# Key tiles in two halves of 64 rows in a fused sparse attention and long convolution

## The chip, the cores and the metric

The kernel runs on one core of a Trainium2 chip. The metric is the device time of one execution in microseconds (us), as the median of several. TensorE (PE) multiplies matrices, VectorE (DVE) and ScalarE (ACT) work element by element, GpSimd (POOL) and SyncE (SP) here mostly issue transfers. A matmul on TensorE has a stationary operand, loaded ahead as weights, and a moving one that streams through; its result goes to PSUM, which the program uses as eight banks of 512 32-bit columns.

## What is computed

An attention with 8 global keys and a local window of 96, and then a gated long convolution. Sizes: B = 4 batches, H = 8 heads, S = 768 positions, D = 64.

```python
scores = (q @ k.T) / sqrt(D)
rel = pos[:, None] - pos[None, :]
is_global = pos[None, :] < 8
is_local = (rel >= 0) & (rel < 96)
dist = where(is_global & ~is_local, 96, abs(rel))
a = softmax(where(is_global | is_local, scores - slope[h] * dist, -1e9))
x = heads_side_by_side(a @ v)                      # (4, 768, 512)
x1, x2, x3 = split(x @ w_proj)
conv = irfft(rfft(x2, axis=1) * rfft(filter_fft, axis=0), axis=1)
out = (x1 * conv * x3) @ w_out
```

So a query needs at most 96 local keys and 8 global ones.

## The kernel before

**Attention.** Keys are cut into seven tiles of 112 rows. Each tile stands in 128 partitions: the 8 global rows first (8 more rows are zero), then 112 keys of its own. A key can be seen by queries up to 95 positions after it, so a tile of 112 keys meets 112+96 = 208 query columns (the last tile 96). For each head pair `scores` (L681) multiplies the transposed keys `KT` (64 rows of one head, 128 columns) with 208 columns of the transposed queries `QT`: L711. The two heads of a pair stand in rows 0 to 63 and 64 to 127. ScalarE takes the exponential into `E` (L739), VectorE multiplies by a mask of decay and window (L751). In batch 0, where the masks come late, the distances are instead added on TensorE before the scores, as products with a diagonal matrix of slopes (`biases`, L686 to L699).

`values` (L754) then works on query tiles that begin at the same places as the key tiles, 112 apart and 128 wide: seven tiles, each with one product with its own key tile (L769) and one with the tile before (L774), 128 rows and 65 columns (64 of v and a column of ones for the sum). VectorE takes the reciprocal (L799) and scales into `xn` (L793); `transpose_x` (L804) turns it on TensorE (L815) or the transfer engines turn it (`crossed_x`, L822), into `xT`. The queries and keys are transposed on TensorE too: in 16 bits by `turned` (L661, L668), the first tiles of batch 0 in 32 bits by `turned32` (L629, L635), some in batch 3 by transfers (`crossed`, L651).

**Loads.** GpSimd's queue loads q, k and v tiles with a change of type (`load_rows`, `load_run`, `load_q`); the first q and k tiles come in 32 bits on SyncE's and ScalarE's queues (`first_tiles`). The global rows of v are copied to all tiles on SyncE's queue (`load_global`), in batch 0 by VectorE or ScalarE from rows that were loaded apart (`first_rows`, L1148).

**Convolution.** Gates (L860), projections (L934), a forward transform (L622), products with the filter's spectrum, an inverse transform (L959, L962), and the output projection (L986), all with weight tiles of 128 x 128.

**Order.** The methods record operations with the tiles that they read and write. `Plan.schedule` (L152) places them in the order that the string `ORDER` (L40) writes out by hand or by a planner: number of the operation, engine, PSUM banks. Each engine works strictly through its own part of that list. A word such as `i17b0` is 17 matmuls on an idle tile (`busy`, L300), at the start.

Of the kernel before, what the change touches and what calls it, by code (L numbers as in the profile page):

```python
# [16 lines left out]
P = 128  # L17
NG = 8
KL = 112
LO = P - KL  # L20
HUGE = 1.0e5
# [19 lines left out]
4V 0S 1A 2S 3A 30V 9G 32A 31A 14V 13V 11V 10A 33V 22G 34V 23V 60A 62A 12V 27V 5V 65A 36G 39G 19S 35A 15V 25V 24G 63A  # L41
16V 40G 18V 42G 41G 59A 45G 28V 8V 26V 46G 48G 29A 47G i17b0 74P0 75V 61A 70P1 72P2 71V 68P3 69V 84P45 64A 106P0 76P1
37G 58A 92P67 73A 79A 78A 93P 88P23 77V 94P 85P 38G 108P1 89P 49G 86P 107A 66V 90P 95A 44G 43G 109V 112P0 113V 87A
110P1 111V 80P67 81P 82P 20V 91A 51G 67V 120P01 83A 114P45 121A 152P2 153V 50G 154P3 155V 118P67 158P0 115A 159V 119A
156P2 157V 17V 116P45 21V 117A 160P67 161A 162P23 163A 96P45 97V 98V 101P01 166P67 167A 164P45 122P23 52G 102V 103V
123V 127P01 104P6 124V 128V 53G 129V 7G 217P7 165A 105A 99P4 168P23 125P6 130P5 258G 100V 218A 126A 212P4 131A 173P01
137P5 132P6 169V 170V 171P2 213A 219V 220V 221A 174V 175V 176P7 138P3 259G 172A 357P0 214V 215V 133P2 134A 267G 266G
216A 224P6 177V 199V 198V 206V 139V 385P7 184P4 358A 55G 135V 255G 189P5 140A 141V 386V 179P7 225A 257G 355P3 256G
264G 226A 183P0 265G 359A 6A 353P1 191A 201V 143P5 227V 181A 136V 194P7 56G 57G 185A 200V 202V 356V 383P0 228V 229A
205V 260G 186A 354V 208V 230A 223V 361P23 145A 203V 196A 367P45 362A 364P67 384V 178P1 207V 148P0 365A 295P2 204V 360V  # L50
368A 180V 396P45 150A 296A 397A 390P67 209V 210V 211V 187V 363V 370P01 371A 391A 293P3 294A 270G 369V 291P2 280P0 366V
387P67 222V 292A 398V 388A 231V 232V 233V 234V 393P45 299P3 300A 394A 54G 281A 282P2 283A 429P1 273G 306P3 307A 278P6
279A 147P7 149A 286P2 372V 261S 235V 236V 272G 287A 389V 142P3 433P6 434A 271G 431P7 144A 263G 430A 485G 237V 373P45
262S 151V 268G 297P2 298A 240P6 484G 241A 182V 193P3 195A 374V 432V 238P2 239A 392V 243P6 244A 269G 375V 395V 378P01
486G 379V 380V 435P45 436A 487G 197V 438P23 439A 404P67 405V 146V 376P0 496G 406V 245P1 246A 377V 437V 581P4 284P5
285A 444P23 445A 441P67 442A 407P1 188P0 488G 582V 399P45 381P2 408A 440V 585P3 274G 190V 400V 401V 446V 583P0 382A
586V 252P67 254A 253A 275G 276G 495G 584V 402P1 403A 447P45 489G 490S 443V 613P7 614A 248P23 448V 494G 587A 249A 304P6
305A 452P01 410P7 250A 412A 500G 247V 712G 449V 450P2 453V 454V 425P6 451A 251V 501G 455P3 659P7 456V 502G 427A 493G
302V 660A 595P01 589P45 498G 478V 590A 596A 592P23 593A 588A 414P6 458P7 499G 727G 468P4 416A 301V 661P5 308V 711G
460A 303V 242V 729G 594V 409P0 657P1 658V 611P2 309V 288V 612A 289V 424P6 426A 428V 477V 479V 290V 411A 470A 662A  # L60
473P1 475A 420P7 422A 415P6 413V 312P4 480V 313A 320P5 725G 417A 324P1 472P0 321V 474A 669P23 325A 598P67 599A 523P4
481V 714G 510P1 670A 316P5 314P0 192V 511A 600V 672P23 621P67 317V 524A 715G 482V 812P1 315A 591V 673A 322P4 323A 622A
310P0 311A 813V 730G 814A 418V 419P5 318P1 319A 597V 506P4 507A 421V 491S 463P5 465A 624P67 618P01 619A 666P23 457P4
667A 519P5 674V 625A 483V 508P0 663P23 881S 615P67 713G 326V 327V 328V 329V 623V 330V 520A 664A 462P1 423V 509A 620V
720G 728G 497G 616A 521P5 492G 606P23 505G 333V 334V 464A 467P0 469A 522A 607V 601P67 466V 277G 602V 608V 459A 626V
350P1 810P5 514P0 665V 351A 716G 347P4 603A 503G 835S 671V 525P1 526A 348A 476V 344P2 717S 722G 811V 837S 504G 527P5
345A 515A 528A 617V 668V 632P67 331V 604P4 605A 678P23 532P0 633V 634V 533A 679V 512P5 513A 680V 332V 808P1 627P67
628V 882S 534P0 675P45 676V 609P2 809A 629V 535A 610A 635P1 335P3 677V 630P2 631V 529V 636A 721G 836S 471V 336A 724G
530V 883S 821P01 822A 818P67 819A 820V 815P45 816A 726G 880S 723G 838S 516V 338P3 839V 652P2 654A 681S 339A 642P6 644A
817V 648P7 531V 846P45 517V 682S 840P23 683S 650A 847A 518V 823V 824P01 825A 826V 647P6 841A 643P7 645A 638P4 640A  # L70
719G 827P01 828V 884V 341P5 829V 342A 649A 646V 653P7 849P01 850A 536V 732G 537V 461V 651V 705V 891P45 343S 892A
888P23 704V 851V 637P6 544P0 689P1 707V 639A 655A 545A 548P4 731G 691A 549A 550P6 542P5 893V 842V 540P7 543A 706V 352S
538P0 539A 552P1 553A 695P4 551A 641V 700P0 541A 702A 708V 697A 690P1 830P67 546P0 692A 848V 685P4 684P1 831V 832V
889A 687A 843P23 693V 890V 709V 885P67 340S 547A 844A 894P45 733P0 895A 886A 554V 710V 896V 718S 750P2 855P45 856V
# [1174 lines left out]
```

## Time and profile before

| | |
|---|---|
| median of 3 runs | 168.94 us (168.76 to 168.98) |
| profiled execution | 168.69 us, its span 166.8 us |
| TensorE busy in the span | 160.3 us, 1,621 matmuls |
| VectorE busy | 152.9 us, 336 instructions |
| ScalarE busy | 144.9 us, 302 instructions |
| GpSimd busy | 73.6 us, 99 instructions |
| granted TensorE clock | 1.000 |

The span goes from the first to the last instruction on the core; the rest of the execution's time lies around it. "Busy" of TensorE includes the overlap of matmuls that follow each other, so a full row there is not yet an engine at its peak. The groups that belong to attention on TensorE, with mean length of one:

```profile
L711 PE MATMUL bank<-QT,KT 64*128 64x208 f16 x192 | 13.6, 251 | 0.9 <-DVE KT L306 0.7 <-DVE xT L306 0.2
...
L668 PE MATMUL bank<-ident,kn 128*128 128x128 f16 x88 | 6.9, 219 | 0.0
...
L815 PE MATMUL bank<-ident,xn 128*128 128x128 f16 x72 | 6.3, 219 | 0.0
```

### The profile page before, as it was taken

How to read it: one execution, taken by the hardware profiler on the slowest of the kernel's cores; microseconds unless marked ns; L12 is line 12 of the kernel's file. 1: busy time of each engine (PE TensorE's matmuls, PEld its weight loads, DVE VectorE, ACT ScalarE, POOL GpSimd, SP SyncE). 2: the span in 40 equal slices, each digit the busy share in tenths (PEclk: the TensorE clock that was granted, in tenths of full speed). 3: DMA queues.
4: the chain of work that ended last, by engine and by line, in shares of the span. 5: the costliest groups of instructions: out<-in, count | busy, mean ns of one | idle time of the engine just before them, and what ended most of it. 6: DMA issues, size and time to landing. Idle time of an engine off the chain costs nothing.

```text
span 166.8 us, 4251 instructions
## 1 busy us (share of the span) xinstructions
PE 160.3 (96%) x1621; PEld 99.8 (60%) x1621; DVE 152.9 (92%) x336; ACT 144.9 (87%) x302; POOL 73.6 (44%) x99
## 2 busy tenths in 40 slices
PE   7999999999999999999999989999999999999990
PEld 2566787664567876666457746765744844575430
DVE  5898979999999999999999979999999999999950
ACT  4589979999999998999999998999896788696731
POOL 7999999973889934999570000000000000000000
PEclk9999999999999999999999999999999999999999
DMA  5999999999999999999999990804052104300685
GB/s 121 193 141 127 130 171 166 169 208 181 169 164 154 155 150 63 92 140 149 158 157 130 125 130 19 265 5 118 17 132 51 63 4 181 137 0 0 246 317 194
DMA packets 92916, 22.06 MB, mean 132 GB/s; under 512 B 85760, under 2 KB 89824, under 8 KB 92896
## 3 DMA queue, kind: packets, MB, share of 16 engines
q0 software_dynamic: 75952, 11.95, 100.9%
q1 hardware_dynamic: 14864, 9.33, 23.9%
q10 hardware_dynamic: 2080, 0.52, 1.7%
q8 instruction: 12, 0.20, 0.5%
q14 instruction: 8, 0.07, 0.1%
HBM read 24.94 MB, written 6.29 MB: 187 GB/s over the span
## 4 chain that ended last, share of the span: by engine, by line
PE 58%; DVE 33%; issue 4%; DMA 3%; ACT 0%; DVEq 0%; SPq 0%
PE bank L860 15%; PE bank L986 9%; DVE E L751 8%; PE bank L934 6%; PE bank L959 4%; PE bank L302 4%; DVE xn L793 4%; PE bank L698 3%; DMA KT<-kn 3%; PE bank L711 3%; PE bank L668 3%; PE bank L622 3%; PE bank L769 2%; DVE g L871 2%; PE bank L774 2%
## 5 line engine op out<-in xcount | busy, mean ns | idle before, releaser
L860 PE MATMUL bank<-xT,w 128*128 128x384 f16 x256 | 47.9, 326 | 0.0
L739 ACT ACTIVATE E<-bank 128x832 f16<-128x832 f32 (+2 forms) x64 | 42.8, 759 | 1.1 <-PE bank L711 1.0
L860 PEld LDWEIGHTS <-w 128*128 128x128 f16 x256 | 23.6, 98 | 15.4 <-issue 0.7
L322 POOL DMA_DIRECT2D kn<-in_k_dram x27 | 22.5, 848 | 6.7 <-PE bank L668 4.8
L322 POOL DMA_DIRECT2D vn<-in_v_dram x28 | 24.0, 865 | 2.2 <-DMA w<-in_moe_w_proj_dram 0.9
L986 PE MATMUL bank<-wo,y 128*128 128x512 f16 x96 | 22.9, 379 | 0.1
L751 DVE TENSOR_TENSOR E<-E,mask 128x832 f16<-128x832 f16 (+1 forms) x36 | 21.7, 622 | 0.0
L322 POOL DMA_DIRECT2D qn<-in_q_dram x21 | 18.8, 904 | 3.5 <-PE bank L934 3.2
L310 ACT ACTIVATE ot<-bank 128x512 f32<-128x512 f32 x22 | 12.8, 615 | 5.9 <-PE bank L986 3.8
L793 DVE TENSOR_TENSOR xn<-bank,rc 128x512 f16<-128x512 f32 (+1 forms) x22 | 16.8, 766 | 0.6 <-DVE rc L799 0.2
L310 ACT ACTIVATE ab<-bank 128x512 f16<-128x512 f32 x24 | 14.6, 655 | 1.2 <-PE bank L934 1.2
L869 ACT CAST g<-bank 128x384 f16<-128x384 f32 x30 | 14.5, 523 | 1.2 <-PE bank L860 1.2
L769 PEld LDWEIGHTS <-E 128*128 128x128 f16 x224 | 14.0, 97 | 2.3 <-issue 0.4
L769 PE MATMUL bank<-vn,E 128*128 128x65 f16 x224 | 15.3, 193 | 0.0
L310 ACT ACTIVATE x<-bank 128x384 f16<-128x384 f32 x26 | 13.5, 528 | 2.0 <-PE bank L860 1.3
L986 PEld LDWEIGHTS <-y 128*128 128x128 f16 x96 | 9.1, 98 | 10.1 <-DVE y L1066 0.2
L774 PE MATMUL bank<-vn,E 128*128 128x65 f16 x192 | 15.1, 193 | 0.0
L711 PE MATMUL bank<-QT,KT 64*128 64x208 f16 (+1 forms) x224 | 14.0, 244 | 0.9 <-DVE KT L306 0.7
L306 ACT CAST X<-bank 128x512 f16<-128x512 f32 x24 | 14.2, 643 | 0.3 <-PE bank L622 0.2
L306 ACT CAST eo<-bank 128x384 f16<-128x384 f32 x29 | 13.4, 542 | 0.3 <-PE bank L962 0.3
L774 PEld LDWEIGHTS <-E 128*128 128x128 f16 x192 | 13.2, 97 | 0.5
L711 PEld LDWEIGHTS <-KT 64*128 64x128 f16 x224 | 8.7, 94 | 6.4 <-issue 2.5
(148 smaller groups left out, 337.4 us busy)
## 6 DMA issues: line engine op xcount, KB each, us to landing
out_dram<-ot SPq DMA_DIRECT2D x24, 256.0 KB, 2.4
vn<-in_v_dram POOLq DMA_DIRECT2D x28, 112.0 KB, 5.4
kn<-in_k_dram POOLq DMA_DIRECT2D x27, 112.0 KB, 5.2
qn<-in_q_dram POOLq DMA_DIRECT2D x21, 128.0 KB, 5.6
w<-in_moe_w_proj_dram POOLq DMA_DIRECT2D x4, 256.0 KB, 5.7
g<-in_moe_filter_fft_dram POOLq DMA_DIRECT2D x1, 768.0 KB, 10.2
ot<-in_q_dram ACTq DMA_DIRECT2D x2, 256.0 KB, 6.6
w<-in_moe_w_proj_dram POOLq DMA_DIRECT2D x1, 512.0 KB, 7.2
```

Source lines behind the costliest of these rows:

```text
L306: {"A": nc.scalar.copy, "V": nc.vector.tensor_copy, "G": nc.gpsimd.tensor_copy}[e](out, in_)
L310: self.nc.scalar.mul(out, in_, c)
L322: return self.g.op(eng, 0.57 + 0.00035 * nbytes[0] if eng == "G" else 0.5, lambda _: e.dma_start(dst, src), w=w, r=r, nbytes=nbytes, name= ...
L711: nc.tensor.matmul(bs[hh].f32()[:, off:off + w], self.KT[hs, hp, P * m:P * m + P], self.QT[hs, hp, KL * m:KL * m + w], start=(off == 0 and ...
L739: nc.scalar.activation(dst, src(), Act.Exp, scale=self.scale)
L751: g.op("V", dve(w, 2), lambda _: nc.vector.tensor_mul(eo, eo, mk), r=[("mask", 2 * hp), ("mask", 2 * hp + 1)], w=[("E", hp, gi)], name="ma ...
L769: nc.tensor.matmul(o[:, n, hh], ef[:, at:at + P], vt[:, t, 2 * hp + hh, 0:D + 1], start=first, stop=(t == 0), skip_group_check=True)
L774: nc.tensor.matmul(o[:, n, hh], ef[:, at:at + P], vt[:, t - 1, 2 * hp + hh, 0:D + 1], start=False, stop=True, skip_group_check=True)
L793: nc.vector.tensor_mul(to, o[:, :, :, 0:D].rearrange("p i (t h) d -> p i t h d", h=2), rc.rearrange("p i (t h) o -> p i t h o", h=2).to_br ...
L860: nc.tensor.matmul(bk.f32()[:, 0:h], self.w[:, c, o + P * j:o + P * j + P], self.xT[:, c, h * s:h * s + h], start=(c == 0), stop=(c == 3))
L869: first = g.op("AV", {"A": act(h), "V": 0.0005}, lambda e: nc.scalar.copy(x3, pts[1].f32()[:, 0:h]) if e == "A" else None, use=[pts[1]], w ...
L986: nc.tensor.matmul(bk.f32(), y[:, c, P * t:P * t + P], self.wo[:, c, :], start=(c == 0), stop=(c == 3))
```

## The change

Each tile of 112 keys is now held as two halves of 64 rows: 8 global rows and 56 keys of its own, the second half with its keys first and the global rows last. A half meets 56+96 = 152 query columns, which begin where its own keys begin. In tiles 1 and 4 (`SWAP`) the halves are stored in the other order. Scores become four products of 64 x 64 weights, two heads by two halves, into four quarters of two banks; the values become products of 64 rows, one head pair on the upper half and another on the lower, alternating, in two passes (`values` and `values2`). Query tiles for the values are now six, 128 apart. All transposes of q, k and x of 16 bits are two products of 64 rows instead of one of 128. The groups of key tiles are (0,1,2), (3,4), (5,6). The masks, distances and zeroed gaps follow the new layout; v tiles 1 and 4 are loaded in two transfers; the global rows of v are copied on SyncE's queue in every batch. `ORDER` is a new list, which begins the attention of batch 0 with q tile 3 and k tile 2, and uses 12 idle matmuls at the start and two later.

```diff
-    N, LAST, STEP = 208, 96, 224
-    GRP = [(0, 1), (2, 3), (4, 5, 6)]
+    N, LAST, STEP, GAP, LEAD = 152, 96, 272, 120, 56
+    GRP = [(0, 1, 2), (3, 4), (5, 6)]
+    QG = [(0, 1), (2, 3), (4, 5)]
+    SWAP = (1, 4)
...
+        self.at = [[KL * t + HL * (1 - y if t in self.SWAP else y) for y in range(2)] for t in range(7)]
...
     def load_rows(self, what, dst, src, b, t):
+        parts = [(NG, lo, n)] if what[0] == "kn" or t not in self.SWAP else [(NG, lo + HL, HL), (64, lo, HL)]
...
+    def load_global(self, vt, s):
+        for y in range(2):
+            lo = (P - NG) * y
+            self.load("S", vt[lo:lo + NG], vt[NG:2 * NG, 0:1].to_broadcast(
+                [NG, 7, self.H, self.VD]), [("vng", s, y)], (NG * 7, 16 * self.VD), "vglobal",
                 r=[("vn", s, 0), ("vn1", s)])
...
     def turned(self, what, ts, buf):
             for x, t in enumerate(ts):
                 for i in range(4):
-                    nc.tensor.transpose(b.f16()[:, 512 * x + P * i:512 * x + P * i + P],
-                                        buf[:, t, 2 * i:2 * i + 2, :], self.ident)
+                    for y, b in enumerate(bs):
+                        ps, o = slice(64 * y, 64 * y + ks[y]), 256 * x + 64 * i
+                        nc.tensor.transpose(b.f16()[:, o:o + ks[y]], buf[ps, t, 2 * i:2 * i + 2, :], self.ident[ps, ps])
...
     def scores(self, hp, gi, near=False):
                 for hh in range(2):
                     hs = slice(64 * hh, 64 * hh + 64)
-                    nc.tensor.matmul(bs[hh].f32()[:, off:off + w],
-                                     self.KT[hs, hp, P * m:P * m + P],
-                                     self.QT[hs, hp, KL * m:KL * m + w],
+                    for y in range(2):
+                        ks, q0 = P * m + 64 * y, self.at[m][y]
+                        nc.tensor.matmul(bs[hh].f32()[64 * y:64 * y + 64, off:off + w],
+                                         self.KT[hs, hp, ks:ks + 64], self.QT[hs, hp, q0:q0 + w],
...
     def values(self, j, c, slot):
+        def run(_, x):
+            todo = [[(hh, n, t) for hh in range(2) for n, t in z] for z in parts]
+            for k in range(max(map(len, todo))):
+                for i, y in ((0, x), (1, 1 - x)):
+                    (hh, n, t), hp, ps = todo[y][k], 2 * j + i, slice(64 * y, 64 * y + 64)
+                    at = self.STEP * t + self.LEAD + P * ts[n] - self.at[t][y]
+                    nc.tensor.matmul(
+                        o[i][:, n, hh], self.E[hp][ps, hh, at:at + P], vt[ps, t, 2 * hp + hh, 0:D + 1],
...
+        g.op("P", cost, lambda _: run(_, 0), acq=bs, r=es + vs, w=[val], name="values")
+        g.op("P", cost, lambda _: run(_, 1), use=bs, r=es + vs, w=[val], name="values2")
...
     def transpose_x(self, j, c):
                 for n, t in enumerate(ts):
-                    o = step * i + KL * n
-                    nc.tensor.transpose(tx[:, o:o + P], self.xn[:, t, 2 * j + i], self.ident)
+                    for y, b in enumerate(bs):
+                        ps, o = slice(64 * y, 64 * y + 64), 128 * i + 64 * n
+                        nc.tensor.transpose(b.f16()[:, o:o + 64], self.xn[ps, t, 2 * j + i], self.ident[ps, ps])
```

Counted in the built programs, TensorE's matmuls go from 1,621 to 2,582; those of the convolution are the same.

## The prediction, made before the result was known

> **What bounds the kernel now.** I read the page first, then the waits of TensorE, then stretches of time, then the order in time at the places that the change touches.
>
> ```profile
> span 166.8 us, 4251 instructions
> ...
> PE 160.3 (96%) x1621; PEld 99.8 (60%) x1621; DVE 152.9 (92%) x336; ACT 144.9 (87%) x302; POOL 73.6 (44%) x99
> ```
>
> Three engines are nearly full, so the page alone doesn't say which one sets the pace. The list of what TensorE waited for does, with the stretches (columns: stretch, length, busy time of each engine, clock, DMA):
>
> ```profile
> PE bank L302 <- DVE idle L372: 1.2, 1, 1.2
> PE bank L711 <- DVE KT L306: 0.7, 1, 0.7
> PE bank L711 <- DVE xT L306: 0.2, 1, 0.2
> ```
>
> ```profile
> 30.00:60.00 30.00, 30.00 (x349) 19.54 (x348) 29.49 (x70) 29.73 (x60) 23.86 (x29) 1.00 2.09 171
> 60.00:90.00 30.00, 29.75 (x297) 18.61 (x296) 29.57 (x60) 29.25 (x65) 20.85 (x25) 1.00 1.90 128
> 90.00:120.00 30.00, 29.31 (x367) 19.72 (x363) 28.80 (x61) 28.51 (x61) 0.00 (x0) 1.00 0.76 101
> 120.00:160.00 40.00, 40.00 (x242) 22.08 (x241) 38.48 (x76) 32.03 (x74) 0.00 (x0) 1.00 0.30 100
> ```
>
> From 30 to 160 us TensorE is busy 129.06 of 130 us. Matmuls overlap, so busy could still hide slack; their pitch (from start to start) tells. These lines are in order of time (start, length, engine, line, weight tile as rows*columns, count):
>
> ```profile
> 29.32 0.50 PE L455 MATMUL bank<-ident,fwd 128*128 128x128 f16 x6
> ...
> 29.75 0.30 PE L458 MATMUL bank<-ident,fwd 128*64 128x128 f16 x4
> ```
>
> ```profile
> 61.29 0.61 PE L668 MATMUL bank<-ident,kn 128*128 128x128 f16 x8
> ...
> 61.83 0.53 PE L711 MATMUL bank<-QT,KT 64*128 64x208 f16 x8
> ...
> 62.53 0.35 PE L711 MATMUL bank<-QT,KT 64*128 64x208 f16 x4 [0.17 <-DVE xT L306]
> ...
> 62.82 2.12 PE L860 MATMUL bank<-xT,w 128*128 128x384 f16 x12
> ```
>
> Eight L668 in 0.61 us, the last one 0.219: a pitch of 0.39/7 = 56 ns at 128 columns. Twelve L860: (2.12-0.326)/11 = 163 ns at 384. So a matmul costs 0.417 ns a column and 2.5 ns: 29.6 ns at 65 columns, 89 at 208, 176 at 416. L711's two heads stand in rows 0-63 and 64-127 and run together: a pair takes 89 ns, not twice that. Summed by this law over the instruction order, all matmuls after the warm-up (L302) stream 146.7 us; the first starts at 7.5 and the last at 162.1 us.
>
> **A cost that no group shows.** The L668 group ends its pitch at 61.29+8x0.056 = 61.74, but L711 starts at 61.83; L711's last pair is through at 62.53+2x0.089 = 62.71, L860 starts at 62.82. About 0.1 us is lost where the shape of the weight tile changes, 64*128 against 128*128, both ways. By the trace's nanoseconds it is 92 to 97 in 40 of the 42 such places (the other two waited for something too). From 128*128 to 128*64 (L455 to L458) it is 93, and back 99. Before has 48 such places in its instruction order: 4.6 us. So of the 154.6 us from the first to the last matmul, 146.7 are stream, 4.6 changes of shape, and only 3.3 waiting: TensorE's own stream is the bound.
>
> **The change part by part**, as TensorE's time.
>
> *Removed.* Scores L711: 96 pairs of 208 columns at 89.2 ns and 16 of 96 at 42.5: 9.24 us. Bias L698: 8 pairs of 208, 20 of 416, 8 of 96: 4.57. Values L769 and L774: 416 x 29.6 = 12.31. Transposes of q and k, L668: 160 x 55.8 = 8.93; of x, L815: 72 x 55.8 = 4.02; in 32 bits, L635: 16 at (1.91-0.273)/15 = 109 ns, 1.75. Sum 40.82.
>
> *Added*, by counts in the new instruction order. Scores are fours of 64*64 tiles: 96 of 152 columns and 16 of 96. No row shows four together. Low bound: they stream as one, 65.8 ns. High: L458's first pair, whose matmul lasted 243 ns and not 219, so 24 ns of a 64-column weight load were exposed, each time: 90 ns, +2.7 us in all. L458 had just come through a change of shape, and its second pair lasts 219 again; so I take 65.8, and 24 ns at each of the 35 entries into that shape: 7.00+0.84. Bias: fours, 8 of 304 columns, 8 of 152, 4 of 96: 1.73. Values: 896 matmuls of 64 rows, 448 pairs. Low bound 29.6 ns a pair, high 59 (one after the other); L698's pairs of 96 columns, the nearest row, start 42 ns apart, which is their streaming, so I take 29.6: 13.26. Transposes: 172 pairs of 64 columns at 29.2, 5.02; of x, 64 pairs, 1.87; in 32 bits, 12 pairs at 56 and four at 96 ns, 1.05. Sum 30.77. So the streams save 10.05 us.
>
> *Changes of shape.* Scores are 64*64 now, values and transposes 64*128, everything of the convolution 128*128, and the new order weaves them closely (a run of four L960 between two runs of twelve scores, for example). The new order has 163 such places, 115 more: 118 between 128 rows and 64, 39 between the two shapes of 64 rows, and the few of L447 to L466. 115 x 0.096 = +11.04. Those 39 are the weak point: bounds 0 and 3.7 us; I take the full price, as L455 to L458 also kept its rows and changed its columns alone.
>
> The Trainium skill bears on this: "TensorEngine Tiling (Array Packing)", section Key Properties, says that changing the tiling mode, not merely the tile, drains the engine, and lists 64x64 and 64x128 as two modes. By it the 39 places cost the full 3.7 us, by the most hopeful reading of the rows nothing; the trace agrees with the rule wherever it shows a change, at 92 to 99 ns.
>
> *Filler.* Two of the warm-up matmuls now stand in mid-run: 2 x 0.216 = +0.43. Twelve and not seventeen at the start fill a wait and count nothing.
>
> *Start.*
>
> ```profile
> 7.52 1.91 PE L635 MATMUL bank<-p,ot 128*128 128x128 f32 x16
> ```
>
> ```profile
> L322 POOL DMA_DIRECT2D qn<-in_q_dram x3: 888/893/895, 4.3 to 8.4; - x3
> ...
> DMA to landing us min/median/max: 4.0/4.4/4.7
> ```
>
> Now the first work is L635 on tiles that SyncE and ScalarE asked for. In the new order it is the transposes of q tile 3, GpSimd's second load, then k tile 2; L635's successors are queued behind. GpSimd's preparation before its loads is about as long, so the load goes out at 4.3 and lands at 8.7: 1.2 us later. The new first v tile then has to cross a second DMA (its eight global rows copied to all tiles on SyncE's queue, in place of L1148's copies), and all values wait for that. Bounds 0 (the stage waits for copies anyway) to 1.5; I take +0.9. VectorE's new zeroing of E (four copies of 1,440 elements) hides in that wait.
>
> *Relief elsewhere.* ScalarE's exponentials shrink from 2,688 to 2,016 elements a head pair: by L739's rows (0.815 ns an element, 209 ns each) 48.6 us to 39.8. L751's masks: 22.4 to 18.7. xn (L793): seven tiles a batch to six, -2.2. On engines that TensorE doesn't wait for this is worth at most the 0.94 us not busy between 30 and 160; I take -0.3. GpSimd gets eight more loads (two half tiles of v a batch), 8 x 0.865 = 6.9 us; it ends near 83 us and had 8 us of waiting for buffers that TensorE still held, which hides them.
>
> *Sum:* -10.05+11.04+0.43+0.9-0.3 = +2.0 us. The profiled execution took 168.69 (span 166.8 and 1.9 around it): 170.7. The median shown is 0.25 above it, 168.94: 171.0.
>
> **Rivals.**
>
> *A change between the two 64-row shapes is free, since the split of the rows stays.* Then 39 x 0.096 = 3.7 us fall away: 167.3, faster. It decides from about 21 of the 39 free. For it: before shows no such place. Against: L455 to L458 also kept its rows, and paid.
>
> *Small matmuls don't pair.* 65-column pairs need four instructions, two weight loads and two matmuls, in 29.6 ns. Before never asks for that for long: its values use two, its 96-column pairs four in 42. If 21 ns a matmul is a floor, 448 pairs lose 12.4 ns, 236 lose 12.8, and 96 fours 18: 5.6+3.0+1.7 = +10.3, 181.3; each nanosecond a pair is 0.68 us. For it: L442 and L444, of one column each, start 25 and 28 ns before their successors. Against: the members of a pair start as near as 4 ns.
>
> The Trainium skill, "TensorE: Matmul & The Clock Gate", section "Wait — 56ns, not 53.3ns?", gives a floor of about 25 ns from start to start however small the matmul; taken for each member of a pair that would be an estimate of 50 ns a pair, and some 14 us more. The pairs of 96 columns, 42 ns for two, already go under it, so it gets no more weight than the row gave.
>
> *TensorE only looks like the bound, VectorE's 92% paces it.* Its work falls by 3.7+2.2 us and the end with it: 163. Against: the three waits above, 2.1 us in all.
>
> *The four score tiles don't run at once*, so the change doesn't do what it says: at worst two by two, 96 x 66+16 x 42 = +7.0, 178.
>
> **How the numbers follow.** Forecast 0.55, own range 169.2 (no late start, 0.9 relief) to 173.7 (score weight loads exposed). Free changes between 64-row shapes 0.17; VectorE 0.05. Pairs with a floor 0.13, fours that don't run at once 0.04, and a start that stalls longer 0.06 (173 to 175). What 0.2% tells from no change is 0.34 us. Faster: 0.17+0.05+0.02 of the forecast's edge = 0.24; same 0.05; slower 0.71. The range reaches down to free changes, 167.0, and up to 8 ns lost a pair, 176.5.
>
> **What would show it.** TensorE still above 95% busy; 96 ns at changes of shape, and as much between scores and values; L798's pairs 30 ns apart, L742's fours 66; the first transposes near 8.7 us; ScalarE and VectorE less busy with no gain from it. I am wrong if the scores-to-values places lose nothing, if pairs take 40 ns, or if the end moves with VectorE's work.

## The result, and the profile after

The changed kernel takes 186.32 us (median of 4 runs, 184.79 to 186.80) against 168.85 us before (168.48 to 168.98): a ratio of 1.102, 95% interval 1.096 to 1.109. It is slower, as forecast, but by 17.5 us and not by 2, and lies outside the range (167.0 to 176.5). The profiled execution took 186.80 us, span 185.0; before it was 168.69. (Ratios in this document leave out executions that took over 1.5% more than the fastest of the same kernel; medians, ranges and the profiled execution of early_q_whole don't, so the two can differ by a per cent.)

The page of the changed kernel (whole span; then busy tenths and granted clock in 40 slices of 4.6 us):

```profile
span 185.0 us, 6176 instructions
PE 169.3 (91%) x2582; PEld 96.1 (52%) x2582; DVE 152.1 (82%) x344; ACT 135.5 (73%) x289; POOL 78.1 (42%) x106
PE   7499965899998999999999799999999999999990
PEclk9965599799999999999999999999999999999999
```

TensorE is at 91%, not above 95%. ScalarE is 9.4 us less busy than before and VectorE 0.8 us, without any gain. And the clock row has something that the kernel before has nowhere after its first microseconds: slices of 5 and 6. The stretches say more (columns as in the prediction: stretch, length, busy time of PE, PEld, DVE, ACT, POOL, clock, DMA):

```profile
10.00:24.00 14.00, 13.29 (x254) 8.49 (x258) 7.99 (x24) 9.08 (x19) 13.85 (x19) 0.51 1.75 137
24.00:34.00 10.00, 5.86 (x254) 4.53 (x247) 3.78 (x10) 5.34 (x11) 9.61 (x13) 1.00 2.21 162
34.00:38.00 4.00, 4.00 (x71) 2.41 (x64) 2.53 (x7) 2.71 (x5) 3.12 (x5) 0.57 1.72 185
60.00:100.00 40.00, 39.47 (x713) 22.13 (x712) 37.49 (x83) 35.57 (x75) 27.48 (x34) 1.00 1.52 106
110.00:140.00 30.00, 29.87 (x473) 17.59 (x472) 28.74 (x60) 21.52 (x53) 0.00 (x0) 1.00 0.26 65
140.00:180.00 40.00, 39.99 (x242) 21.97 (x241) 36.57 (x73) 29.83 (x64) 0.00 (x0) 1.00 0.32 114
```

The same columns of the kernel before, in its first stage:

```profile
10.00:20.00 10.00, 10.00 (x168) 6.96 (x166) 8.79 (x25) 9.50 (x16) 10.00 (x13) 1.00 2.04 131
20.00:30.00 10.00, 9.96 (x169) 7.46 (x164) 8.82 (x21) 8.83 (x17) 10.00 (x14) 1.00 1.93 164
```

From 60 us on TensorE is as full as before, but for one wait of 1.2 us at 105 us. More than half of the loss sits ahead of 40 us: 14 us in which it looks busy at half clock, then 10 us in which it works only 5.86. What it waited for (total, times, longest):

```profile
PE bank L798 <- issue: 4.5, 3, 2.4
PE bank L691 <- DMA qn<-in_q_dram: 2.9, 2, 2.5
```

"issue" is a wait that no semaphore explains. Two of its three places, in order of time:

```profile
26.86 0.37 PE L798 MATMUL bank<-vn,E 64*128 64x65 f16 x13 [1.17 <-issue]
27.16 0.30 PE L727 MATMUL bank<-eo 64*64 64x152 bf16 x8
...
29.71 0.69 PE L798 MATMUL bank<-vn,E 64*128 64x65 f16 x33
32.78 0.28 PE L798 MATMUL bank<-vn,E 64*128 64x65 f16 x7 [2.38 <-issue]
```

Both stand in the middle of one values operation, between two matmuls on tiles that were there. In the same lines the change of shape can be read: the last of the thirteen L798 starts at 26.86+0.37-0.19 = 27.04 and has 0.03 us to stream, L727 starts at 27.16, 0.09 later.

Summed over all matmuls of the two profiled executions, from the first real matmul to the last: streaming 146.44 us before, 138.33 after (-8.1); changes of shape, at up to 96 ns, 4.51 and 15.29 (+10.8); the rest, waits and the surplus at half clock, 3.66 and 17.55 (+13.9). The first real matmul starts at 9.04 and not 7.52 (+1.5). Together +18.1, the whole difference. The first gate matmul (L860, now L882), which closes the first stage, comes at 35.99 us and not 25.39: 10.6 of the 18.1 us are lost by then. By the same sums, the stage between these two matmuls streams 12.3 us and not 15.3, has 3.7 us of changes of shape and not 1.7, and 11.0 us of the rest and not 0.9. Behind it the streams save 5.0 us (131.2 to 126.2), but the changes of shape cost 8.7 more (2.8 to 11.5) and the rest 3.8 more: there the change loses without any help from the clock.

### The profile page after: what moved, and what is told of

It is laid out like the page before. It is cut to its first block, busy times and chain, and to the rows that moved or that the text cites. A ratio compares the mean times of both kernels' runs of the same rounds, so it can differ in the third digit from the quotient of the medians.

```text
span 185.0 us, 6176 instructions
## 1 busy us (share of the span) xinstructions
PE 169.3 (91%) x2582; PEld 96.1 (52%) x2582; DVE 152.1 (82%) x344; ACT 135.5 (73%) x289; POOL 78.1 (42%) x106
## 4 chain that ended last, share of the span: by engine, by line
PE 70%; DVE 11%; POOL 5%; issue 4%; ACT 4%; DMA 4%; POOLq 0%; DVEq 0%
PE bank L882 21%; PE bank L1012 12%; PE bank L960 8%; PE bank L798 7%; PE bank L629 6%; PE bank L985 5%; DMA qn<-in_q_dram 4%; PE bank L742 3%; PE bank L691 3%; POOL kn L329 2%; PE bank L838 2%; DVE E L778 2%; PE bank L727 1%; POOL qn L329 1%; DVE pp L565 1%
## 5 line engine op out<-in xcount | busy, mean ns | idle before, releaser
L882 PE MATMUL bank<-xT,w 128*128 128x384 f16 x256 | 49.7, 330 | 0.0
L772 ACT ACTIVATE E<-bank 128x304 f16<-128x304 f32 (+3 forms) x64 | 34.4, 610 | 6.8 <-PE bank L742 6.7
L329 POOL DMA_DIRECT2D vn<-in_v_dram x36 | 28.2, 796 | 9.0 <-DMA g<-in_moe_filter_fft_dram 2.9
L882 PEld LDWEIGHTS <-w 128*128 128x128 f16 x256 | 22.7, 98 | 15.5 <-issue 0.5
L329 POOL DMA_DIRECT2D kn<-in_k_dram x27 | 22.6, 844 | 10.3 <-PE bank L691 9.7
L798 PE MATMUL bank<-vn,E 64*128 64x65 f16 x896 | 21.0, 193 | 4.8 <-issue 4.5
L798 PEld LDWEIGHTS <-E 64*128 64x128 f16 x896 | 16.6, 95 | 13.0 <-issue 11.3
L778 DVE TENSOR_TENSOR E<-E,mask 128x608 f16<-128x608 f16 (+1 forms) x36 | 18.0, 517 | 0.0
L742 PE MATMUL bank<-QT,KT 64*64 64x152 f16 x448 | 16.3, 246 | 0.9 <-ACT E L772 0.6
L818 DVE TENSOR_TENSOR xn<-bank,rc 128x512 f16<-128x512 f32 x23 | 15.7, 688 | 0.5
L317 ACT ACTIVATE ot<-bank 128x512 f32<-128x512 f32 x21 | 12.4, 614 | 4.7 <-PE bank L1012 4.3
L313 ACT CAST eo<-bank 128x384 f16<-128x384 f32 x29 | 12.8, 509 | 2.2 <-PE bank L988 1.5
L742 PEld LDWEIGHTS <-KT 64*64 64x64 f16 x448 | 10.0, 114 | 8.4 <-issue 6.3
L1012 PEld LDWEIGHTS <-y 128*128 128x128 f16 x96 | 8.8, 98 | 10.3 <-DVE y L1092 0.5
L313 ACT CAST X<-bank 128x512 f16<-128x512 f32 x23 | 13.0, 595 | 1.0 <-PE bank L629 1.0
L629 PE MATMUL bank<-ab,fwd 128*128 128x512 f16 x40 | 11.5, 382 | 0.0
L985 PE MATMUL bank<-inv,X 128*128 128x256 f16 x64 | 11.3, 273 | 0.1
## 6 DMA issues: line engine op xcount, KB each, us to landing
g<-in_moe_filter_fft_dram POOLq DMA_DIRECT2D x1, 768.0 KB, 10.1
```

The costliest lines, as they stand in the source:

```text
L313: {"A": nc.scalar.copy, "V": nc.vector.tensor_copy, "G": nc.gpsimd.tensor_copy}[e](out, in_)
L317: self.nc.scalar.mul(out, in_, c)
L329: return self.g.op(eng, 0.57 + 0.00035 * nbytes[0] if eng == "G" else 0.5, lambda _: e.dma_start(dst, src), w=w, r=r, nbytes=nbytes, name= ...
L629: self.nc.tensor.matmul(b.f32(), self.fwd[:, f], src(i, t), start=(n == 0), stop=(n == len(terms) - 1))
L742: nc.tensor.matmul(bs[hh].f32()[64 * y:64 * y + 64, off:off + w], self.KT[hs, hp, ks:ks + 64], self.QT[hs, hp, q0:q0 + w], start=(off == 0 ...
L772: nc.scalar.activation(dst, src(), Act.Exp, scale=self.scale)
```

## The experiments

The first theory was: TensorE waits 2.5 us for q after only twelve warm-up matmuls, this lowers its clock, and the half clock costs up to 8.5 us. The second: the waits called "issue" are for instructions. Each set of runs shared runs of the kernel before on its own chip; their medians are 169.71, 170.00, 169.49 and 169.55 us, so ratios compare best. "Late" sums the waits that no semaphore explains at every 256th of TensorE's instructions, weight loads and matmuls counted: 192, 448, 704 and so on (the ones above 0.5 us). after_again is the changed kernel a second time: its trace differs by 1.7 us in the first gate matmul and by 2.8 us in the late instructions, so smaller differences between single traces show nothing by themselves.

| run | us, median (range) | ratio, 95% interval | first gate, us | half clock after the first rise, us | late, us |
|---|---|---|---|---|---|
| changed kernel | 186.32 (184.79-186.80) | 1.102, 1.096-1.109 | 36.0 | 17.1 | 5.0 |
| long_warmup | 183.98 (180.66-185.94) | 1.071, 1.060-1.082 | 33.2 | 10.2 | 1.9 |
| short_start | 184.21 (183.50-186.13) | 1.087, 1.079-1.095 | 35.0 | 13.7 | 2.7 |
| before_short_warmup | 169.84 (168.79-172.69) | 0.999, 0.996-1.003 | 26.0 | 0 | 0 |
| whole_transposes | 183.31 (183.20-184.34) | 1.082, 1.075-1.089 | 34.5 | 6.8 | 1.4 |
| filler_in_slow_window | 185.41 (185.10-185.93) | 1.090, 1.085-1.096 | 35.1 | 13.7 | 3.3 |
| filled_wait | 187.82 (185.87-190.92) | 1.096, 1.089-1.103 | 34.8 | 3.4 | 3.4 |
| fewer_changes | 192.73 (192.16-194.06) | 1.135, 1.129-1.141 | 33.6 | 20.5 | 6.9 |
| before_reordered | 181.71 (181.25-185.03) | 1.068, 1.063-1.074 | 30.3 | 3.4 | 0 |
| after_again | 186.44 (184.04-188.53) | 1.088, 1.080-1.097 | 34.3 | 20.5 | 2.2 |
| early_q | 182.56 (180.97-185.20) | 1.074, 1.066-1.082 | 32.3 | 10.2 | 1.1 |
| early_q_whole | 184.90 (182.59-185.82) | 1.087, 1.077-1.096 | 35.8 | 13.7 | 2.4 |
| dense_pairs | 200.37 (200.00-200.75) | 1.183, 1.174-1.192 | 25.4 | 13.7 | 12.1 |
| held_clock | 188.46 (187.47-191.37) | 1.108, 1.098-1.118 | 36.7 | 10.2 | 6.0 |
| alternating | 190.80 (190.14-191.14) | 1.126, 1.119-1.133 | 25.4 | 0 | 0 |
| grouped | 182.80 (181.95-183.54) | 1.079, 1.072-1.086 | 25.5 | 0 | 0 |

**Is it the wait at the start?** Three runs of the first set vary what stands at the start.

```diff
-30G 31A 29V i12b0 81P01 8V 27A 87P23 50G
+30G 31A 29V i24b0 81P01 8V 27A 87P23 50G
```

> The changed kernel with 24 warm-up matmuls instead of twelve, nothing else: twelve more at 0.216 us fill the 2.53 us that TensorE waits for q at 6.5 to 9.0 us. Theory clock (that wait is what brings the half clock granted at 10.38 to 24.03 and at 34.27 to 37.68 us): the granted clock stays at 1.00 from about 7 us to the end, and a good part of 17.1/2 = 8.5 us comes back, 186.3 to 178-182. Rival load-bound start (in the first 25 us TensorE waits for copies anyway, and the clock costs little): the clock may stay full, but the time stays within 1.5 us of 186.3. Rival activity (the clock falls because the matmuls of the first 25 us are small and spaced, not because of the wait): half clock stays at about 10.4 us and the time stays. On the stalls that no semaphore explains (1.34 us at 26.85, 2.55 at 32.77, 1.16 at 105.41; before TensorE's instructions 704, 960 and 3520, counting weight loads and matmuls): theory instruction supply says that they stand again before instructions 704 and 960, which are now 24 instructions earlier in the program, and not at 3520 unless small matmuls run up to it; rival data says that they stand at the same values operations as now.

Of the wait 1.2 us are left, the clock is up from 4.2 us, and it falls all the same, from 17.9 to 28.1 us (page, clock row):

```profile
PEclk9999558999999999999999999999999999999999
```

The ratio falls from 1.088-1.102 to 1.071. The two executions that it rests on took 180.66 and 182.81 us, about the upper end of the theory's 178 to 182, but not for its reason, since the clock did not stay up. On the instructions the theory of supply was right in kind: the unexplained waits now stand before instructions 960 and 1,216, the latter in the middle of gate work (L882, 1.33 us at 36.0 us), so at steps of 256 in the count and at other operations. The one before 704 did not come again.

```diff
-i12b0 81P01 8V 27A 87P23
+i16b0 77P67 83P4 75P01 8V 27A 84A 76A 87P23 81P01
```

> The changed kernel with the order of its start put back nearer to that of the kernel before: sixteen warm-up matmuls, then the 32-bit transposes of q1, k0 and q0, whose loads land first, and only then k tile 2 and q tile 3. Theory clock: TensorE's first real matmul starts near 7.5 us and not 9.0, no wait above 1 us before it, the granted clock stays at 1.00, and the time falls like that of the long warm-up or up to 1.5 us more: 177 to 182. Rival load-bound start: the first matmul is earlier but the first gate matmul (35.99 us in the changed kernel) stays within 1 us, and the time within 1.5 us of 186.3.

The first real matmul comes at 7.04 us. Then TensorE waits 1.8 us ahead of the transposes of q tile 3, by the trace for ScalarE's copy of earlier queries out of a bank (L313). The clock falls at 12.7 us, and the first gate matmul comes at 35.0 us, between the two traces of the changed kernel (36.0 and 34.3). No gain from the earlier start is shown.

```diff
-48G 29A 47G i17b0 74P0
+48G 29A 47G i8b0 74P0
```

> The kernel before with eight warm-up matmuls instead of seventeen, nothing else, so that TensorE has nothing to do for some 2.5 us before its first real matmul at 7.5 us. Theory clock: the same half clock shows in this kernel, in stretches of 3.4 us from about 10 us on, and it becomes 3 to 9 us slower, 172 to 178. Rival activity (only the small matmuls of the changed kernel lower the clock): the clock is back at 1.00 by about 10 us and the time stays within 1 us of 168.9.

In the kernel before, a wait of 2.1 us at this place costs nothing (page):

```profile
span 167.6 us, 4233 instructions
PEclk9999999999999999999999999999999999999999
```

Its clock rises at 9.7 us and stays. The first theory falls: the clock falls with most of the wait filled (long_warmup), and with a wait left open it stays up once it has risen (here).

**Is it what TensorE does?** Four matmuls of 512 columns go into the slow stretch at two places:

```diff
-91P67 102P 129P01 14V
+91P67 102P i4b0 129P01 14V
-94P 127P01 104P
+94P i4b0 127P01 104P
```

> The changed kernel (twelve warm-up matmuls) with four matmuls of 512 columns on whole 128x128 tiles put ahead of the transposes of two k tiles, at about 12 and 13 us, inside the stretch of half clock (10.38 to 24.03 us). Theory activity (the clock follows how much of a 3.4 us window the array is streaming: the windows after which it fell held 0.41 to 1.34 us of streaming at full clock, those after which it stayed 1.20 or more, and at half clock it came back after windows of 2.33 us or more and stayed down at 1.20 to 2.41): eight matmuls lift the windows from 10.4 us on, the clock comes back near 14 us and not at 24, and the time falls by 1 to 5 us although 1.7 to 3.4 us of matmuls are added. Rival gap (only a wait of TensorE above about 1 us lowers the clock, for a fixed stretch): half clock stays until about 24 us, and the time grows by 0 to 3.4 us.

The stretches of this run (columns as above):

```profile
12.00:15.00 3.00, 3.00 (x26) 1.17 (x26) 0.40 (x1) 0.97 (x3) 3.00 (x5) 0.52 1.75 130
15.00:25.00 10.00, 8.14 (x216) 5.56 (x218) 6.46 (x18) 6.37 (x12) 10.00 (x14) 1.00 1.85 149
25.00:32.00 7.00, 6.53 (x173) 4.54 (x165) 3.29 (x8) 4.45 (x9) 6.60 (x9) 0.51 2.25 164
```

The clock is back at 14.9 us and not at 24, as the theory of activity said and a fixed stretch after a wait can't give. It falls again at 25.1, and the time gains nothing clear: 185.4 us, ratio 1.090, where the changed kernel has 1.088 and 1.102.

```diff
-229P1 109P 32V 105A 110A 125P67
+229P1 109P 32V 105A 110A i10b6 125P67
```

(on top of the long warm-up)

> The long warm-up with ten more matmuls of 512 columns (2.16 us) ahead of the transposes of q tile 5, where that kernel waited 2.34 us for the load of q and after which its clock fell at 17.9 us. Theory activity and theory gap both say that the clock stays at 1.00 from 4 us to the end; the first gate matmul then comes at 29 to 31 us instead of 33.2 and the time falls from 182-184 to 178-181. Rival load-bound start: the clock stays full, but values wait for v or for ScalarE's exponentials instead, the first gate matmul moves by less than 1 us, and the time stays within 1 us of the long warm-up.

The clock stays at 1.00 from 5.8 to 33.1 us, and the first gate matmul still comes at 34.8, 1.6 us later than in long_warmup; the ratio is 1.096 and not 1.071. Neither theory of the clock expected that: the added matmuls take 2.2 us themselves, q comes 0.8 us later still, TensorE then waits 1.4 us for a bank that VectorE's work on the sine table (L429) holds, and 1.8 us for instructions. The rival "load-bound start" is right that other waits follow, but the time missed its 1 us as well: it is some 4 us longer.

**Loads of q.** GpSimd's q5 and q4 change places with v tile 0 and k tile 5, on top of the long warm-up; the second run adds whole transposes (below); the changed kernel ran again beside them.

```diff
-51G 40G 15V 42G 38V ... 87P23 50G 55G 48G 49G 56G
+51G 40G 15V 49G 38V ... 87P23 50G 48G 42G 55G 56G
```

> The changed kernel as it is, beside the others of this set on one chip, since differences of 1 to 3 us are to be read: 184 to 187 us, half clock in the first 40 us and waits of 1 to 2.6 us before TensorE's instructions 704, 960 and 3520 (the middle of values), give or take one of them.

Its waits stand before instructions 960 (0.6 us) and 1,216 (1.6 us), and not before 704 and 3,520: which block comes late changes between executions of one program, but it is again a wait at one of these counts.

> The long warm-up with GpSimd's loads of q tiles 5 and 4 in third and second place nearer to the start (the order of the kernel before puts them early too): q5 where v tile 0 stood, v tile 0 and k tile 5 behind q4. Theory late load (the 2.34 us that TensorE waits for q at 15 to 17 us, and with it the fall of the clock at 17.9 us, come from q's load standing behind three tiles of k and one of v): no wait above 1 us before the transposes of q, granted clock 1.00 until at least 28 us, first gate matmul at 29 to 31 us instead of 33.2, the time 3 to 4 us below the long warm-up: 179 to 181. Rival load-bound start (all loads of batch 0 are needed anyway): the wait moves to another load of about the same length (k tile 3 or v), the first gate matmul moves by less than 1 us.

The wait for q is gone, but TensorE now waits 1.84 us for v's copied rows at 20.7 us; the first gate matmul gains 0.9 us on the long warm-up where 2 to 4 were expected, less than two traces of one kernel differ by, and the ratio none (1.074 and 1.071). The rival holds. This run has the clearest evidence that the clock falls without a wait. Windows of it, cut where the clock can change:

```profile
9.00:12.40 3.40, 3.37 (x84) 2.51 (x84) 2.89 (x14) 3.32 (x10) 3.40 (x5) 1.00 2.13 136
12.40:15.80 3.40, 3.17 (x78) 1.87 (x72) 1.83 (x6) 2.40 (x4) 3.39 (x6) 1.00 1.84 118
15.80:19.20 3.40, 3.01 (x69) 2.04 (x62) 2.63 (x10) 3.15 (x8) 3.40 (x6) 0.50 1.42 126
```

TensorE is busy 3.17 of 3.40 us in the second row and is put on half clock in the third: no wait did that.

**Which work counts.** In the traces the granted clock changes only on a grid of 3.413 us, in which TensorE can stream 8,192 columns at full clock (0.417 ns a column, as in the prediction). I added up the columns of the matmuls of each window, each weighted with the part of 128x128 that its tile covers (rows rounded up to 32, 64 or 128), 32-bit ones twice. Over all 17 profiled executions, more than 800 windows: after a window with a share of 0.37 or more the clock is full, after one below it is half; six windows break this, all between 0.359 and 0.384. Busy time doesn't separate them: its best limit leaves 35 windows wrong. The middle row of early_q above holds a share of 0.37, just under the limit. The kernel before holds 0.77 or more in every window up to 60 us once warm; the changed kernel holds, from 7 us on, 0.27, 0.34, 0.22, 0.31, 0.37, 0.37, 0.51, 0.29, 0.41, 0.81. In that stage small tiles that change shape every few matmuls, with a wait now and then, often fill less than a third of the array.

**Do late instructions cost what they seem to?** The transposes of q, k and x go back to whole tiles, on top of the long warm-up (and of early_q):

```diff
-                    for y, b in enumerate(bs):
-                        ps, o = slice(64 * y, 64 * y + ks[y]), 256 * x + 64 * i
-                        nc.tensor.transpose(b.f16()[:, o:o + ks[y]], buf[ps, t, 2 * i:2 * i + 2, :], self.ident[ps, ps])
+                    o = 512 * x + P * i
+                    nc.tensor.transpose(bs[0].f16()[:, o:o + rows], buf[0:rows, t, 2 * i:2 * i + 2, :],
+                                        self.ident[0:rows, 0:rows])
```

> The kernel with the long warm-up, with the transposes of q, k and x as whole tiles of 128 (k: 120) rows into one bank, as the kernel before has them, instead of pairs of 64 rows; the rest and the order as they are. Theory change of shape (96 ns each also counts in the total): 129 changes and not 163, -3.3 us, against 6.0 us more stream: 2.7 us slower than the long warm-up. Rival changes hidden (they lie in waits that would be there anyway): 5 to 6 us slower. Rival instruction supply pays (236 fewer matmuls, so fewer instructions asked for in the first 40 us): the stalls before 704 and 960 shrink, and it comes out 0 to 2 us faster instead.

> The same with the transposes of q, k and x on whole tiles of 128 rows. Theory change of shape alone: 2.7 us slower than early_q (6.0 us of stream against 34 changes). Theory instruction supply: 236 matmuls and as many weight loads fewer, so shorter waits before every 256th instruction; as far as these waits shrink (1 to 3 us in the traces so far) it comes out equal to early_q or up to 1 us faster.

The first pair differs by 1.1% (ratios 1.082 and 1.071), the second by 1.2% (1.087 and 1.074), with intervals that overlap: about 2 us slower, between the 2.7 of the shapes alone and the gain hoped for from fewer instructions. These two don't decide it. The next does: dense pairs on a tile of zeros, in the kernel before, once where the DMA engines are busy and once where they are not.

```diff
+    def dense(self, n, bs):
+        for _ in range(n):
+            for y, b in enumerate(bs):
+                ps = slice(64 * y, 64 * y + 64)
+                self.nc.tensor.matmul(b.f32()[:, 0:65], self.idle[ps, 0:P], self.idle[ps, 0:65], start=True, stop=True)
...
-363V 370P01 371A
+363V j256b01 370P01 371A
...
-897P01 349S
+j256b01 897P01 349S
```

> The kernel before with 256 pairs of 64-row matmuls of 65 columns on a tile of zeros (what values are made of in the changed kernel: two weight loads and two matmuls a pair, 1,024 instructions) put in twice, at about 39 us, where the DMA engines are busy all the time, and at about 118 us, where they are mostly idle. Their own stream is 256 x 29.6 ns = 7.6 us each time. Theory instruction supply (a block of 256 instructions is asked for only when the block before it is entered, and takes about 6 us to come while the DMA engines are busy and about 3 while they are not): the first 256 pairs take 16 to 24 us, the second 10 to 14, in steps with a wait before every 256th instruction counted from the start (at 192, 448, 704, ...), and the clock falls in the first. Rival data (the waits in the middle of values were for tiles, not for instructions): 7.6 us each time, no wait inside, 184 us in all.

In order of time:

```profile
38.86 2.50 PE L314 MATMUL bank<-idle 64*128 64x65 f16 x153
45.21 2.88 PE L314 MATMUL bank<-idle 64*128 64x65 f16 x128 [3.86 <-issue]
50.58 3.70 PE L314 MATMUL bank<-idle 64*128 64x65 f16 x128 [2.50 <-issue]
55.41 3.02 PE L314 MATMUL bank<-idle 64*128 64x65 f16 x103 [1.12 <-issue]
...
138.39 2.57 PE L314 MATMUL bank<-idle 64*128 64x65 f16 x157
141.89 2.12 PE L314 MATMUL bank<-idle 64*128 64x65 f16 x128 [0.94 <-issue]
145.35 2.12 PE L314 MATMUL bank<-idle 64*128 64x65 f16 x128 [1.34 <-issue]
148.80 1.67 PE L314 MATMUL bank<-idle 64*128 64x65 f16 x99 [1.33 <-issue]
```

Nothing here waits for data, yet TensorE stops after every 128 matmuls, 256 instructions with their weight loads. A block takes 3.45 us from start to start where the DMA engines are nearly idle (14 GB/s), 4.8 and 5.4 where they are busy (147 GB/s; there up to 3.5 us of a block is streaming at half clock), and 256 pairs take 12.1 and 19.6 us instead of 7.6. In the busy part the clock falls too, from 46.3 to 59.9 us, after a window that held a share of 0.28. The traces show packets of 16,384 bytes on the instruction queue; in the changed kernel one starts when TensorE enters a block, at once or up to 3.7 us later, and TensorE goes on 2.2 to 2.4 us after its start. Both sizes are as expected, and the data theory falls.

By the Trainium skill ("Runtime: NRT & Kernel Launch", section Instruction fetch mechanics) instructions are refilled in blocks of 256, and crossing a boundary is "mostly hidden". The block agrees; hidden it is only where 256 instructions take longer than those 3.5 to 6 us.

**Does a change of shape cost its 96 ns in the total?** First the order after the first gate matmul was rearranged by a small model of the engines (durations from the traces), once for the changed kernel with the long warm-up and once, as a control, for the kernel before. The edit is the order alone, some 860 words of it.

> The long warm-up with the same operations, the instruction order after the first gate matmul rearranged so that work on tiles of one shape stands together: 118 changes of shape where the long warm-up has 163, all of the 45 after the first gate matmul. Theory change of shape: the stretch from the first gate matmul to the last matmul falls from 143.0 us by 45 x 0.096 = 4.3 us and by up to 1.5 us of small waits, to 137 to 139.5; the time falls by as much. Rival changes hidden or other engines bound: less than 1.5 us.

> Control: the kernel before with its own operations, the order after its first gate matmul rearranged in the same way and with the same effort; it has 53 changes of shape, about as many as before (48), so no gain can come from these. If waits are as few as the prediction read (0.94 us not busy between 30 and 160 us), it gains 0 to 2 us from 168.9; if it gains 3 us or more, the order of the kernel before held waits that the matmul pitch hides, and the comparison of the two tilings has to allow for the order.

Both came out far slower, so neither says what it was made for. In fewer_changes the changes of shape did fall, from 15.2 to 10.9 us in the sum over the trace, but transposes that now stand together use up instructions faster (page and waits of TensorE, from 33 us):

```profile
PEclk9996579889999957999999999999999999999998
```

```profile
PE bank L691 <- issue: 5.3, 2, 2.8
```

During the second of these waits, 2.95 us up to 68.2, the window ends with a share of 0.26, and the clock is at half from 67.5 us for 6.8 us. In before_reordered TensorE waits 4.4 us for loads of k that the model thought were there. The model knew neither the supply of instructions nor the clock nor the late loads, so these two runs leave open what a better order would do. Then the same question with nothing else in play:

```diff
+            mm(bs[0].f32(), z[:, 0:P], z, start=True, stop=True)
+            mm(bs[1].f32(), z[0:64, 0:P], z[0:64], start=True, stop=True)
```

> The kernel before with 32 matmuls of 128 rows and 32 of 64 rows, 512 columns each, on a tile of zeros, put in at about 118 us, one of the one and one of the other in turn: 62 changes of shape more than with the same matmuls in two groups. Theory: 62 x 0.096 = 6.0 us more than grouped, in the total time. Rival (the gap at a change hides in work that waits anyway, or shrinks when the change is known ahead): less than 3 us.

> The same 64 matmuls, first the 32 of 128 rows, then the 32 of 64 rows: 64 x 0.216 = 13.8 us of stream and two changes more than the kernel before, 183 to 184.

Alternating takes 8.0 us more (8.2 by the profiled executions). In the trace the starts of alternating, then of grouped:

```profile
119.46 0.38 PE L313 MATMUL bank<-idle 128*128 128x512 f16 x1
119.77 0.39 PE L314 MATMUL bank<-idle 64*128 64x512 f16 x1
120.09 0.39 PE L313 MATMUL bank<-idle 128*128 128x512 f16 x1
120.42 0.39 PE L314 MATMUL bank<-idle 64*128 64x512 f16 x1
120.73 0.39 PE L313 MATMUL bank<-idle 128*128 128x512 f16 x1
```

```profile
117.82 7.07 PE L313 MATMUL bank<-idle 128*128 128x512 f16 x32
124.82 7.08 PE L315 MATMUL bank<-idle 64*128 64x512 f16 x32
```

0.32 us apart instead of 0.216: 104 ns a change, 6.5 us for the 62. The other 1.6 us do not belong to them: alternating starts its first added matmul at 119.46 and grouped at 117.82, though the programs are the same up to there (some 0.7 us of it go to a wait for v at 48.4 us). Behind the last added matmul the difference stays at 8.1 us to the end, so the 6.5 us are paid in full, and the prediction's 96 ns was, if anything, low.

**All at once.** q5 and q4 one or two places early, v where it was, and 19 matmuls of 512 columns in seven places between 11 and 20 us:

> The long warm-up with GpSimd's loads of q5 and q4 one or two places earlier, v tile 0 left where it is, and 19 matmuls of 512 columns (4.1 us at full clock) spread over seven places between 11 and 20 us. Theory that the causes add up: the granted clock stays at 1.00 from 5 us to 30 us, no wait above 1 us before the transposes of q, the first gate matmul at 29 to 31 us (long warm-up 33.2, early q 32.3), and the time 178 to 181. Rival next bound (each cause relieved uncovers the next: v with its copied global rows, ScalarE's and VectorE's work on the tables, instructions that come late): full clock, but the first gate matmul at 32 to 35 us and the time within 2 us of early_q's 182.6.

The first theory falls and the rival is right in kind: the clock stays at 1.00 until 31.3 us, no wait for q is left above 1 us after 9 us, and yet the first gate matmul comes at 36.7. The rival's own numbers are missed too, 32 to 35 us for that matmul and a time within 2 us of early_q's. Of the 27.7 us from the first real matmul to there, 4.5 are idle matmuls; and instructions come late at two places:

```profile
28.73 0.23 PE L798 MATMUL bank<-vn,E 64*128 64x65 f16 x3
30.38 0.75 PE L798 MATMUL bank<-vn,E 64*128 64x65 f16 x37 [1.42 <-issue]
...
34.15 0.32 PE L466 MATMUL bank<-ident,fwd 128*64 128x128 f16 x1
36.30 0.42 PE L466 MATMUL bank<-ident,fwd 128*64 128x128 f16 x3 [1.83 <-issue]
```

Holding the clock with matmuls that compute nothing did not pay: by the ratios (1.108 and 1.071) this run is some 6 us slower than long_warmup, with 6.0 us of late instructions and 10.2 us at half clock behind 31.3 us. No version of the changed kernel came near 169 us.

## Why the prediction was wrong

The side was right, the size was not: +2.0 us forecast, +18.1 between the profiled executions. By its own steps:

- **The bound.** "TensorE's own stream is the bound" holds after as before from 60 us on, if the changes of shape are counted with it. In the first stage it no longer holds: from the first real matmul to the first gate matmul the kernel before streams 15.3 of 17.9 us, the changed kernel 12.3 of 27.0.
- **The step that failed** is to carry this bound over to the changed kernel's first stage: the sum prices every matmul at full clock, as in the kernel before, and leaves +0.9 for the start and -0.3 for small waits where the rest of that stage grew by 10.1 us. "Twelve and not seventeen at the start fill a wait and count nothing" is not what failed: before_short_warmup shows that fewer warm-up matmuls alone count nothing in the kernel before. What counts is the work behind them: after windows with shares of 0.22 to 0.34 of the array the changed kernel spends 17.1 us at half clock. The surplus, over what the matmuls and changes would have taken at full clock, sums to 6.0 us.
- **The term that was missing** is the supply of instructions. The count of matmuls was in the prediction (448 pairs of values), the stream of each too, but not that 256 instructions need 3.5 to 6 us to come: 1.3+2.5+1.2 = 5.0 us in the profiled execution, 2.2 in after_again.
- **Start.** First real matmul +1.5 us, +0.9 taken, bound 1.5: right in kind. That q's later tiles stood behind three of k and one of v wasn't priced; early_q took that wait away, and the time did not move measurably. The other small waits add about 2.9, where -0.3 was forecast.
- **Changes of shape.** +10.8 us measured, +11.04 forecast. The weak point, the places between 64x64 and 64x128, paid in full (87 to 100 ns each at full clock where nothing else was waited for). At half clock a change takes 110 to 145 ns beside the stream at that clock. By the Trainium skill ("TensorEngine Tiling (Array Packing)", Key Properties) a change of tiling mode drains the engine; the trace agrees.
- **Streams.** -9.6 forecast with the filler, -8.1 measured. Pairs of values run together, 31 ns each (14.0 us, forecast 13.3), fours of scores with their weight loads 8.1 us (7.8). The rival of unpaired matmuls is out, and so are free changes of shape, fours one after the other, and VectorE as the bound: it is busy for 152.1 us where it was for 152.9, and the end came 18.1 us later.

The sum, against what was taken: streams +1.5, changes -0.3, start +0.6, half clock +6.0, instructions +5.0, other waits +3.2: 16.0 us of the 16.1 that the profiled execution missed by. This is an account of one execution and not what each cause would give back: after_again has 20.5 us at half clock, 2.2 us of late instructions and ends 2.8 us sooner. None of the three signs of being wrong that the prediction named came about; it had none for the clock or for the instructions. The side does follow from its terms: streams and changes of shape alone come to +2.7 us, where +1.4 was forecast. The other 15.4 us were not in it.

What stays open: how half clock, late instructions and loads share the first stage, since each one relieved uncovered the next. What that stage holds beside streams and changes of shape is 11.0 us in the changed kernel, 9.2 in after_again, 8.0 in long_warmup, 7.5 in early_q, and, with the added matmuls, 10.3 in filled_wait and 11.2 in held_clock, against 0.9 in the kernel before; no run of the changed kernel came near that. Open too is what delays a block of instructions by up to 3.7 us in some places and not in others with the DMA engines equally busy; and whether an order of the changed kernel exists that keeps the changes of shape few and the instructions in time.

## What to carry to other kernels

When large matmuls are cut into small ones, price three things beside the stream: about 0.1 us for each change of tile shape, the instructions (256 of TensorE's, weight loads included, per 3.5 us at best and per 5 to 6 under heavy DMA), and the share of the array that each 3.4 us window streams, since below about 0.37 the next window runs at half clock. Look at the stage in which the small work stands together, and not only at the sum over the kernel. A busy row of 90% at a clock of 0.5 is not a busy engine, and in three runs filling it with idle matmuls gained nothing.

## What the runs showed of the hardware

- The granted clock follows the streamed share of the array in windows of 3.413 us, limit between 0.36 and 0.38 (more than 800 windows, 17 executions), in both directions, and transposes count like other matmuls: with them left out the best limit leaves over 20 windows wrong, not six. By the Trainium skill ("TensorE: Matmul & The Clock Gate", section HAM oscillation — how this bites in real kernels) it is gaps of more than about 3.4 us that must be avoided. Here the clock fell after a window in which TensorE was busy for 93% (early_q, 12.4 to 15.8 us), so the measurement asks for more than that rule.
- In dense_pairs TensorE got 256 instructions in 3.45 us, 13.5 ns each, with the DMA engines nearly idle, and in 4.8 to 5.4 us while they were busy; a pair of 64-row matmuls, four instructions in 30 ns, asks for nearly twice the first rate.
- A late block of instructions can lower the clock of the next window too: 2.95 us late, and 6.8 us at half clock from the window's end on (fewer_changes, 65 to 74 us).
